# A fused attention and MLP kernel on one core: PSUM banks from one table, batch 0's leftover q and k through GpSimd, and remade instruction orders

## The chip, the core and the metric

The kernel runs on one core of a Trainium2 chip. The metric is device time in microseconds (us), as the median of several runs of one kernel. Engines are written PE (TensorE matmul), PEld (its weight loads), DVE (VectorE), ACT (ScalarE), POOL (GpSimd) and SP (SyncE). A run is called slow below when it lies more than 1.5% above the fastest run of the same kernel, and fast otherwise; comparisons use fast runs alone.

## The reference

Two stages, f32 in and f32 out. First a Performer attention with 128 random features, for 8 batches, 8 heads, 576 rows and 64 columns per head; then an MLP with a sigmoid gate over all 4608 rows.

```python
def phi(x):                                    # x is q or k, scaled by 64 ** -0.25
    proj = einsum('bhsd,md->bhsm', x, omega)   # 64 -> 128 features
    h = proj - sum(x * x) / 2
    h = h - max(h, axis=-1)
    return exp(h) / sqrt(128)

kv  = einsum('bhsm,bhsd->bhmd', phi(k), v);  z = sum(phi(k), axis=2)
num = einsum('bhsm,bhmd->bhsd', phi(q), kv);  den = phi(q) . z + 1e-6
x   = (num / den) as (4608, 512)

h   = x @ w_in                                 # 512 -> 2048
out = (h / (1 + exp(-1.702 * h))) @ w_out      # 2048 -> 512
```

## The kernel before

The program is a graph of some 1,530 operations. Three tables, made beforehand, say how it runs: `ORDER` is the fixed sequence of each engine, `BANK` names the PSUM bank of each accumulation group, and the waits are derived from data, buffers and banks. An engine that waits for one operation holds everything after it in its list.

```python
def schedule(self):
    self.order = {e: [ops[i] for i in ORDER[e]] for e in ENGINES}
    names = iter(BANK)
    for op in ops:
        for gr in op.opens:
            gr.bank = next(names)          # one of H0 H1 O0 O1 P0 P1 S0 S1
    ...                                    # a group waits for the bank's last group

def emit(self, name, eng, sems):
    for op in self.order[name]:
        for n, v in self.waits[op.i]:
            eng.wait_ge(sems[n], v)
        ...                                # then the instructions of op
```

576 rows are four blocks of 128 and a rest of 64, which the kernel calls the *leftover* and packs for all heads into tiles of its own (QL for q and k, VL for v). In batch 0 its q and k come over SP as f32 into QLF and are cast by DVE:

```python
def load_ql(b, key, ckey, after=()):
    pool = b >= QL_SW                      # QL_SW = 2: batches 0 and 1 over SP
    ...
    g.add(POOL if pool else SP, lambda e, dst=dst, so=so: e.dma_start(dst, so), ...)
    ...
    fv = lambda e: e.tensor_copy(out=QL[s][:, :, :, :], in_=QLF[s][:, :, :, :])
```

From there runs a chain that every V group (phi(k) times v, the sum over rows) of the batch needs: transpose on PE, copy to TL, projection with omega, maximum per row (NML, on DVE), exp of it (WWL, on ACT), mask and product with v on POOL (WWM, VPL).

The MLP has two stages for each batch. In stage 1, 16 groups of four 512-column matmuls each go through a tanh on ACT and a multiply on DVE into GT. In stage 2, four blocks of 128 rows accumulate 16 matmuls each; ACT copies a block into one of four output buffers, OS, and SP issues the output.

```python
NQK, NV, NTT, NQP, NVP, NO, NTH, NGT, NOUT = 2, 2, 4, 4, 4, 4, 3, 2, 4
...
gr, os_ = Group(POOL_OF["O" if sbi < 7 else "Oend"], False), m % NOUT
...
g.add(ACT, lambda e, ...: e.activation(out=OS[os_][:, :], in_=at(gr, 0, 512)(), func=ACTF.Copy, scale=0.5), ...)
g.add(SP, lambda e, ...: e.dma_start(dst, OS[os_][:, :]), ..., reads=[("os", os_)], ...)
```

The SP list holds the DMA transposes (TT and TL from loaded q and k, XT from attention's result OO) from batch 2 on.

## Time and profile before

| | before |
|---|---|
| time, median of the runs given at first | 324.06 us (323.75 to 324.21) |
| span of the profiled run | 321.7 us |
| PE busy | 307.4 us (96%) |
| first projection / first V / first stage 1 / first stage 2 starts | 9.48 / 15.85 / 26.50 / 41.44 us |
| last matmul ends | 317.7 us |

The prediction below shows the shares, the stretches, the waits and both ends. Two more places turn out to matter. The first is where the leftover chain of batch 0 ends, in the timeline (start, duration, engine, source line, operation, output from input, form; in brackets the idle time before it and what ended it):

```profile
13.37 1.04 POOL L683 TENSOR_TENSOR VPL<-VL,WWM 128x512 bf16<-128x512 f32 x1
...
15.85 0.42 PE L427 MATMUL PB<-VP,QKP 128*128 128x65 bf16 x8 [0.73 <-ACT QKP L641]
```

The product with v is done at 14.4 us, and what PE waits for before the first V group at 15.85 is an exp on ACT, not the leftover. The second place is the SP queue with the first outputs, in the timeline, and the busy times of the stretch from 100 to 120 us (PE, weight loads, DVE, ACT, POOL, clock, DMA share, GB/s):

```profile
77.70 0.83 SPq L1003 DMA_DIRECT2D out_dram<-OS  x2
78.64 6.08 SPq L762 DMA_TRANSPOSE TT<-QK  x2
```

### The profile page before, as it was taken

The numbers are of one execution on the slowest core, as the hardware profiler recorded it, in microseconds if no ns is written. First come the engines' busy times: TensorE is split into PE (matmuls) and PEld (weight loads), VectorE is DVE, ScalarE is ACT, GpSimd is POOL, SyncE is SP. The second block draws the span as 40 slices with busy tenths as digits, with TensorE's granted clock in tenths as the row PEclk, the third lists the DMA queues.
The fourth block names the chain that finished last, engine by engine and source line by source line (L and its number), as shares of the span: only waits on it lengthen the run. The fifth ranks groups of instructions, "written<-read, shape, count | busy, mean of one in ns | idle before, by whom it ended". The sixth has DMA issues, their size and how long they took to land.

```text
span 321.7 us, 5787 instructions
## 1 busy us (share of the span) xinstructions
PE 307.4 (96%) x2246; PEld 151.2 (47%) x2246; DVE 190.7 (59%) x401; ACT 187.3 (58%) x378; POOL 113.1 (35%) x185
## 2 busy tenths in 40 slices
PE   1798999999999999999999999999999999999994
PEld 1574554445544544454454544454544444444442
DVE  0899985368656784686648745788574533342210
ACT  1789855489178646665658766686545543343231
POOL 6696283627019705933644364031200000000000
PEclk9999999999999999999999999999999999999999
DMA  7999999996889989998999999933022002011005
GB/s 134 241 226 222 207 210 222 151 145 129 209 163 206 226 120 162 245 193 155 141 159 194 207 158 168 151 99 61 2 41 86 0 2 98 33 67 65 33 17 148
DMA packets 84119, 44.20 MB, mean 137 GB/s; under 512 B 54844, under 2 KB 77756, under 8 KB 84092
## 3 DMA queue, kind: packets, MB, share of 16 engines
q0 software_dynamic: 29792, 20.45, 42.0%
q1 hardware_dynamic: 54300, 23.37, 35.4%
q8 instruction: 18, 0.29, 0.4%
q14 instruction: 9, 0.07, 0.1%
HBM read 36.73 MB, written 9.44 MB: 144 GB/s over the span
## 4 chain that ended last, share of the span: by engine, by line
PE 86%; ACT 5%; DVE 5%; DMA 2%; issue 1%; POOL 1%; POOLq 0%
PE HT L427 36%; PE OB L427 34%; PE PB L427 11%; PE SB L427 4%; ACT QKP L641 3%; DMA QK<-in_q_dram 2%; DVE GT L966 1%; DVE NM L631 1%; ACT TH L961 1%; DVE OO L855 1%; ACT QKL L641 1%; POOL QK L478 1%; DVE TT L598 0%; DVE RD L847 0%; PE PB L868 0%
## 5 line engine op out<-in xcount | busy, mean ns | idle before, releaser
L966 DVE SCALAR_TENSOR_TENSOR GT<-TH,HT 128x512 bf16<-128x512 f32 x144 | 97.8, 683 | 80.4 <-ACT TH L961 80.0
L427 PE MATMUL HT<-XT,WIN 128*128 128x512 bf16 x576 | 142.2, 379 | 0.6 <-DVE GT L966 0.3
L961 ACT ACTIVATE TH<-HT 128x512 f32<-128x512 f32 x144 | 86.2, 600 | 82.7 <-PE HT L427 74.9
L427 PE MATMUL OB<-WOUT,GT 128*128 128x512 bf16 x496 | 122.5, 379 | 0.0
L427 PEld LDWEIGHTS HT<-XT,WIN 128*128 128x128 bf16 x576 | 52.7, 98 | 61.5 <-DVE GT L966 7.7
L427 PEld LDWEIGHTS OB<-WOUT,GT 128*128 128x128 bf16 x496 | 45.7, 98 | 53.4 <-issue 3.4
L780 POOL TENSOR_TENSOR VP<-VS,WW 128x512 bf16<-128x512 f32 x32 | 33.5, 1050 | 38.8 <-ACT WW L774 38.7
L641 ACT ACTIVATE QKP<-PB 128x512 bf16<-128x512 f32 x54 | 31.4, 600 | 7.2 <-PE PB L427 4.1
L641 ACT ACTIVATE QKP<-SB 128x512 bf16<-128x512 f32 x56 | 33.0, 606 | 2.8 <-PE SB L427 1.1
L995 ACT ACTIVATE OS<-OB 128x512 f32<-128x512 f32 x31 | 18.6, 599 | 16.7 <-PE OB L427 16.6
L631 DVE TENSOR_REDUCE NM<-SB 128x4 f32<-128x512 f32 x31 | 20.9, 682 | 8.8 <-PE PB L427 7.4
L631 DVE TENSOR_REDUCE NM<-PB 128x4 f32<-128x512 f32 x23 | 15.5, 683 | 6.9 <-PE PB L427 5.3
L427 PE MATMUL PB<-WOUT,GT 128*128 128x512 bf16 x80 | 19.4, 379 | 0.0
L478 POOL DMA_DIRECT2D QK<-in_k_dram x17 | 13.4, 790 | 7.1 <-DMA QK<-in_q_dram 4.2
L789 POOL CAST VP<-WW 128x8 bf16<-128x8 f32 x32 | 7.0, 225 | 24.3 <-ACT WW L774 24.3
L855 DVE TENSOR_TENSOR OO<-PB,RD 128x320 bf16<-128x320 f32 x29 | 13.7, 485 | 0.4
L478 POOL DMA_DIRECT2D QK<-in_q_dram x17 | 13.0, 768 | 0.0
L503 POOL DMA_DIRECT2D QL<-in_k_dram x12 | 7.8, 649 | 13.6 <-DMA TT<-QK 13.6
L427 PEld LDWEIGHTS PB<-WOUT,GT 128*128 128x128 bf16 x80 | 7.8, 98 | 9.5 <-DVE GT L966 0.3
L855 DVE TENSOR_TENSOR OO<-SB,RD 128x320 bf16<-128x320 f32 x24 | 11.5, 482 | 0.3
L532 POOL DMA_DIRECT2D VS<-in_v_dram x12 | 7.8, 661 | 7.2 <-DMA TT<-QK 7.2
L427 PE MATMUL PB<-TT,omB 64*128 64x512 bf16 (+1 forms) x31 | 10.2, 377 | 0.0
(140 smaller groups left out, 285.7 us busy)
## 6 DMA issues: line engine op xcount, KB each, us to landing
out_dram<-OS SPq DMA_DIRECT2D x32, 256.0 KB, 2.8
VS<-in_v_dram POOLq DMA_DIRECT2D x12, 512.0 KB, 6.6
QK<-in_k_dram POOLq DMA_DIRECT2D x15, 256.0 KB, 6.4
QK<-in_q_dram POOLq DMA_DIRECT2D x15, 256.0 KB, 7.3
WIN<-in_moe_w_in_dram POOLq DMA_DIRECT2D x4, 512.0 KB, 10.7
WOUT<-in_moe_w_out_dram POOLq DMA_DIRECT2D x4, 512.0 KB, 17.2
VS<-in_v_dram SPq DMA_DIRECT2D x4, 256.0 KB, 6.4
VS<-in_v_dram SPq DMA_DIRECT2D x2, 512.0 KB, 12.4
```

The costliest lines, as they stand in the source:

```text
L427: return lambda e: e.matmul(o() if callable(o) else o, lhsT=l, rhs=r, **kw)
L478: POOL, lambda e, dst=dst, so=so: e.dma_start(dst, so), 800, key,
L503: POOL if pool else SP, lambda e, dst=dst, so=so: e.dma_start(dst, so), 120, key,
L532: SP if b < V_SW else POOL, lambda e, dst=dst, so=so: e.dma_start(dst, so), 120, key,
L631: lambda e: e.tensor_reduce(out=o, in_=bass.AP(TILE[gr.bank], 0, [[512, 128], [128, 4], [1, 128]]), axis=AX.X, op=ALU.max, negate=True,),
L641: lambda e: e.activation(out=o, in_=view(gr, 0, pat or [[1, 512]])(), func=ACTF.Exp, scale=scale),
L780: lambda e: e.tensor_tensor(out=VP[vs][:, :, 0:64], in0=bass.AP(V, t * 9 * 64 + 64, [[NT * 9 * 64, 128], [64, 8], [1, 64]]), in1=bass.AP(W ...
L789: POOL, lambda e: e.tensor_copy(out=VP[vs][:, :, 64], in_=WW[vs][:, :]), 140, key + K_W + 240,
L855: lambda e, gr=gr, x=x: e.tensor_tensor(out=OO[os_][:, 5 * x : 5 * x + 5, :], in0=bass.AP(TILE[gr.bank], 0, [[512, 128], [65, 5], [1, 64]] ...
L961: lambda e, gr=gr, th=th: e.activation(out=TH[th][:, :], in_=at(gr, 0, 512)(), func=ACTF.Tanh, scale=0.851),
L966: lambda e, gr=gr, th=th, jc=jc: e.scalar_tensor_tensor(out=GT[gi][:, jc, :], in0=TH[th][:, :], scalar=1.0, in1=at(gr, 0, 512)(), op0=ALU. ...
L995: lambda e, gr=gr, os_=os_: e.activation(out=OS[os_][:, :], in_=at(gr, 0, 512)(), func=ACTF.Copy, scale=0.5),
```

## The change

The intent is to gain at the start (more banks, omega sooner, one cast less), to remove the two waits in the middle by orders made with a margin for late transposes and loads, and to shorten the end. Cut to its core:

```diff
-BANKS = dict(b0=<8 banks>, b1=<5>, b2=<5>, bv=<6>, H="H0 H1", O="O0 O1", Oend=<4>)
+BANKS = dict(b0=<8 banks>, b1=<8>, b2=<8>, bv=<6>, H=<8>, O=<8>, Oend=<8>)
-QL_SW = 2
+QL_SP = (1,)              # only batch 1's leftover q and k over SP; batch 0's over POOL, which casts
+TAIL = True
 ORDER = { PE: ... ACT: ... DVE: ... POOL: ... SP: ... }   # all five lists remade (cut)
 BANK  = ...                                               # remade over eight banks (cut)

+    def last_block(gi, key):           # the last 128 rows as two halves of 256 columns
+        for half in range(2):
+            ...                        # 16 matmuls of 256 columns, in 4 groups of 4
+            cut = 128 if half else 256
+            g.add(ACT, ... out=OS[os_][:, 0:cut], in_=at(gr, 0, cut)() ...)
+            if half:
+                g.add(DVE, ... out=OS[os_][:, 128:256], in0=at(gr, 128, 256)() ...)
+            for h in range(2):
+                g.add(ACT if half and h else SP, ... e.dma_start(dst, OS[os_][64*h : 64*h+64, 0:256]) ...)
 # cut: a halved leftover reduction that no batch uses; costs of the planner
```

The cast of batch 1's leftover moves from POOL to DVE in the new orders, and the first memset of the identity too.

## The prediction

> **What bounds the kernel now.** I read the page's shares first, then the busy time by stretch, then the waits of PE, then both ends in the timeline.
>
> ```profile
> PE 307.4 (96%) x2246; PEld 151.2 (47%) x2246; DVE 190.7 (59%) x401; ACT 187.3 (58%) x378; POOL 113.1 (35%) x185
> ...
> 0.00:8.00 8.00, 1.39 (x9) 0.82 (x9) 0.56 (x5) 1.42 (x2) 5.26 (x12) 1.00 0.70 134
> 8.00:16.00 8.00, 6.30 (x60) 4.53 (x60) 6.63 (x20) 6.03 (x16) 5.09 (x9) 1.00 1.33 242
> 16.00:24.00 8.00, 7.88 (x139) 6.27 (x136) 7.28 (x23) 6.89 (x17) 7.33 (x12) 1.00 1.25 226
> 24.00:32.00 8.00, 7.02 (x70) 3.67 (x67) 7.36 (x16) 7.47 (x17) 5.74 (x10) 1.00 1.26 223
> 32.00:40.00 8.00, 7.80 (x89) 4.26 (x88) 7.61 (x18) 7.25 (x17) 2.41 (x4) 1.00 1.24 207
> ...
> 240.00:260.00 20.00, 20.00 (x94) 8.96 (x93) 10.76 (x17) 10.15 (x17) 0.00 (x0) 1.00 0.16 43
> ...
> 310.00:322.00 12.00, 7.71 (x36) 3.33 (x34) 0.00 (x0) 2.98 (x5) 0.00 (x0) 1.00 0.43 111
> ```
>
> The columns after the stretch are PE, weight loads, DVE, ACT, POOL, clock, DMA share, GB/s. PE is at 96%, and from 40 us on it is never idle. But busy PE overlaps itself (a 512-column matmul lasts 379 ns and starts every 216), so I added up, from start to start, what exceeds columns / 2.4 GHz. The 576 + 576 MoE matmuls at 216 ns are 249 us; all PE work is 287 us. Excess after 40 us is 13 us, and almost all of it comes in equal steps that no order removes: 202 ns after each pair of 64-row projections (two run side by side, so this is their own time) and some 104 ns before one. Only two gaps are waits: 0.71 us at 179 us and 0.28 us at 94 us. Before 40 us it is another matter: first matmul at 5.67 us, then 7.2 us of excess to 20 us and 4.5 us to 40 us, of which I estimate 1.3 us as the cold clock and mode steps. So about 16 us are lost at the start, 1 us in the middle, and 4.0 us after the last matmul (317.7 to 321.7). In 8 to 40 us ACT (27.6 of 32 us) and DVE (28.9 of 32) are the full engines: here the kernel is bound by evacuating PSUM, with data still arriving. Only stage 2 of the MoE, whose first group starts at 41.4 us, gives PE work that needs little of either.
>
> ```profile
> PE OB L725 <- DMA QK<-in_k_dram: 5.7, 1, 5.7
> PE SB L725 <- DMA QK<-in_k_dram: 0.9, 1, 0.9
> PE PB L427 <- ACT QKP L641: 0.7, 1, 0.7
> PE HT L427 <- DVE TT L598: 0.6, 1, 0.6
> PE HT L868 <- DVE OO L855: 0.6, 1, 0.6
> ```
>
> These are the waits of PE: first for the q and k loads, later for ACT and DVE. Nothing else over 0.6 us is in that list.
>
> ```profile
> 0.73 0.81 SPq L491 DMA_DIRECT2D QLF<-in_q_dram  x1
> ...
> 1.60 0.62 SPq L491 DMA_DIRECT2D QLF<-in_k_dram  x1
> ...
> 2.91 0.46 SPq L446 DMA_DIRECT2D om_f<-in_omega_dram  x1
> ...
> 7.55 0.20 DVE L449 CAST om_raw<-om_f 128x64 bf16<-128x64 f32 x1 [6.58 <-DMA om_f<-in_omega_dram]
> 7.66 0.42 DVE L509 CAST QL<-QLF 128x512 bf16<-128x512 f32 x1
> ...
> 9.48 0.63 PE L427 MATMUL PB<-omB,TT 128*128 128x128 bf16 x4
> ...
> 316.02 0.60 ACT L995 ACTIVATE OS<-PB 128x512 f32<-128x512 f32 x1 [2.86 <-PE PB L427]
> 317.75 0.60 ACT L995 ACTIVATE OS<-PB 128x512 f32<-128x512 f32 x1 [1.13 <-PE PB L427]
> ```
>
> The timeline of both ends. Omega is fourth in the SP queue, behind two leftover loads and one of v; it holds DVE for 6.58 us, and the first projection starts only at 9.48. At the end one 0.60 us eviction follows the last matmul, then two output issues of 0.51 us one after the other, and the last lands 2.4 us after its issue, at 321.25.
>
> **What the Trainium skill says.** "DMA: Bandwidth & Descriptors", section "Issuing engines are not separate DMA queues": transfers from SP, ACT and GpSimd run on the same 16 engines and interleave. The trace agrees: from 2 us the completions of loads come as one stream, batch 0's q and k by 15.0, its last v at 15.0, the four WIN pieces at 22.7, 31.1, 33.7, 38.8, the WOUT pieces from 36.2 to 46.8, each 1 MB read in 2.6 us. Moving a load to another queue changes its turn, not the end of the stream. The same page, "SWDGE vs HWDGE vs iDMA": a cast during the DMA can only be issued from GpSimd. That is why batch 0's leftovers go there; the trace charges 0.77 us of POOL per such issue, against 0.62 to 0.81 on SP. "PSUM — Partial Sum Buffer", "Specifications (TRN2)", gives 8 banks, and no PSUM access for GpSimd: ACT and DVE alone empty them. In this trace too no POOL row reads one.
>
> **The change part by part.**
> *Bank table.* Before, stage 1 may use only H0 and H1, stage 2 only O0 and O1, attention of batches 1 to 7 five others. Now every group may take any of eight. No instruction is added. A stage 1 group holds its bank for 0.86 (PE) + 0.60 (tanh) + 0.68 (DVE) = 2.14 us plus handovers, against 0.86 us of PE per group: with two banks PE cannot run stage 1 alone at full speed (a group every 1.1 us or more). That matters only where stage 2 is not there to fill, in 26 to 41 us. There ACT and DVE have slack: over 8 to 40 us, 4.4 and 3.1 us. I count a third of the smaller: 1.0 us. After 40 us nothing is to be had from banks.
>
> *Batch 0's leftovers.* Two 128 KB f32 loads leave the head of the SP queue and become the 8th and 9th issues of POOL (counting the identity), and DVE's 0.42 us cast disappears; batch 1's 0.61 us cast moves from POOL to DVE at about 0.42, and one 0.23 us memset too. So DVE's total stays even. Omega is now second on SP, behind one load of v: an estimate from the stream (256 KB in about 1.3 us) lands it near 4 us in place of 7.5. The identity comes after five POOL issues: 1.24 + 5 x 0.77 + 0.3 = 5.4 us. k of pair 0 is the first load and should land near 5.6. So the first projection can start near 7.2 in place of 9.48: 2.3 us earlier for the ACT and DVE work behind it. But they are then fed by a stream whose last q and k of batch 0 still comes near 14 to 15 us, so I count 1.5 us.
> Against it: the leftovers land near 14.6 us (issued at 6.2 and 7.0, behind the rest of batch 0) in place of 5.8. Every V group of batch 0 reads the leftover v, scaled by the leftover k's maxima. Transpose 0.4, copy 0.6, projection 0.4, reduce 0.68, exp 0.2, two POOL products 1.3 and handovers make about 4.3 us, so V starts near 19 against 15.85 now. The new PE order has all batch 0 projections before V and more of batch 1 before the first stage 1 group (position 54 in place of 51), so this is partly covered; I charge 0.5 us.
>
> *New orders.* Batch 1's loads are gated on one q load, which was the fourth POOL issue and landed at 10.55 (POOL stood idle 4.17 us for it). It is now second, so this wait goes; but the DMA stream is full then, so it is worth nothing by itself. In the middle the margin can save at most the two waits, 1.0 us; I count 0.7.
>
> *Leftover split.* The code that halves the leftover reduction needs batch ≥ 1 and batch in (0,): it never runs. The descriptor counts and costs only serve the planner. Both cost nothing.
>
> *Tail.* The last 128-row block is computed as two 256-column halves, 32 matmuls of 108 ns in place of 16 of 216: no PE time, if the 98 ns weight loads keep up. The first half leaves while the second (1.73 us) runs. After the last matmul an eviction of 128 columns on ACT and one on DVE, side by side, take about 0.30 (estimate: half of 0.60) in place of 0.60; the two last issues go to SP and ACT at once, which saves 0.51; half the bytes save perhaps 0.1. Sum 0.9 us.
>
> Together: 1.5 + 1.0 - 0.5 + 0.7 + 0.9 = 3.6 us. 324.06 - 3.6 = 320.5 us.
>
> **Rivals.** (1) The late leftovers decide: V of batch 0 at 19 us or later, the first stage 1 group no earlier than now (26.5). For it speaks that ACT and DVE are short of other work until all loads are in. Then only banks, middle and tail are left, minus a little: about 322.5. (2) The start is better than I count: with all banks ACT and DVE run without a break from 6.5 us. Batches 0 and 1 and stage 1 of batch 0 cost them some 38 us each (my sum: per batch 18 exps of 0.60, 9 reductions of 0.68, about 9 copies of 0.5, 8 products of 0.485 and small ones, 28 us, so 14 each; 16 stage 1 groups of 0.60 + 0.68, 10 each), and half of their slack would become PE work; then 5 us at the start, and 318. Against it stand the serial chain in batch 0 and the load stream, which ends at 46.8 in any order. (3) A shared pool hurts: stage 2 accumulates over four groups and may hold several banks open, and a late transpose then blocks PE, whose order is fixed. The trace shows transposes landing 4.6 us after issue; one such stall a batch would cost 6 us and give 326. The orders were made with margin for just this, so I give it little.
>
> **Range and chances.** The end is sure within some 0.4 us, the middle within 0.7; the start carries the spread, from 0 to 5 us. Hence 317.8 to 323.2. Faster by over 2% needs under 317.6, about 6.5 us: 0.10. Slower by over 2% needs rival 3 on a large scale: 0.01.
>
> **What would show it.** Right: first projection between 6.8 and 7.8 us; first stage 1 group at 24 to 26 us; PE full from about 38; last eviction about 0.3 us and the span ending about 3.1 us after the last matmul; PE work unchanged at 287 us. Wrong: PE waits for DVE or POOL around 17 to 20 us (rival 1), or waits of more than 1 us after 60 us, for a transpose or a bank (rival 3); excess before 40 us, the wait for the first matmul included, under 13 us in place of 17.4 (rival 2; I expect 14 to 16).

## More of the kernel before

```profile
100.00:120.00 20.00, 20.00 (x173) 10.24 (x172) 15.51 (x37) 11.82 (x25) 10.34 (x17) 1.00 1.14 182
```

These two outputs (OS0 and OS3) leave just ahead of the next batch's transposes, and at 100 to 120 us PE is full, with a granted clock of 1.00. One output of batch 0 is late already here: the block in OS2 was evicted at 63.84 us, issued at 90.95 and landed at 93.76, 30 us later. It costs nothing, because the next eviction into OS2 starts only at 105.79.

## The result

| kernel | median us (range, runs) | fast runs against before's, same chip and rounds |
|---|---|---|
| before | 324.13 (323.75 to 324.37, 4) | |
| changed | 327.64 (326.66 to 333.22, 4; the 333.22 is slow) | 1.0092 [1.0063, 1.012] |

The changed kernel is 0.9% slower; the prediction was 1.1% faster and its range ended at 323.2. A ratio here is the mean time of one kernel's fast runs over the mean of the other's fast runs of the same rounds, so it isn't quite the ratio of the medians quoted, nor of all the runs listed (the plain means of experiment 1 would give 1.0114 in place of 1.0103); the brackets are its 95% interval. A fifth run of the changed kernel, 326.31 us and fast, counts in its ratio.

The profile that came with the changed kernel fell in the slow state. I therefore ran it again (first experiment), and show that run's profile. Two cautions on it: it is the longest of its six runs (330.94 us), and 38 of its matmul records are missing, so its PE busy sums are a little low. Both profiles of the changed kernel are thus of long executions (330.94 and 333.22 us); none of a typical one, near 327 us, was taken.

The page's shares and the stretches, against those shown of before:

```profile
PE 307.6 (93%) x2224; PEld 154.8 (47%) x2262; DVE 188.9 (57%) x398; ACT 187.3 (57%) x384; POOL 114.2 (35%) x185
```

```profile
8.00:16.00 8.00, 5.12 (x41) 3.99 (x40) 3.85 (x7) 2.78 (x7) 2.62 (x6) 1.00 1.22 218
16.00:24.00 8.00, 6.09 (x61) 4.09 (x59) 5.17 (x11) 7.52 (x19) 4.98 (x8) 1.00 1.26 243
...
100.00:120.00 20.00, 16.94 (x137) 8.61 (x139) 11.65 (x27) 10.51 (x22) 7.54 (x13) 0.91 0.97 194
```

The work is the same: all matmuls laid end to end by columns, as the prediction counts them, are 287 us before and 287 after (from the complete records of the slow profile). The lost time sits in two places. From 8 to 24 us DVE is busy 9.0 us (3.85 + 5.17) where it was 13.9 (6.63 + 7.28), and ACT in the first eight of these 2.78 where it was 6.03. And the stretch at 100 to 120 us, full before, has holes, at a clock of 0.91. The waits of PE say who is waited for:

```profile
PE SB L569 <- POOL ident L436: 5.6, 1, 5.6
PE SB L429 <- DVE GT L995: 2.9, 1, 2.9
PE PB L754 <- DMA QK<-in_k_dram: 1.7, 1, 1.7
PE PB L754 <- DMA QK<-in_q_dram: 1.2, 1, 1.2
PE HT L754 <- DMA QK<-in_k_dram: 1.0, 1, 1.0
PE OB L429 <- POOL VPL L723: 0.8, 1, 0.8
```

The first is the start-up, as before. The 2.9 us wait for DVE is the hole near 105 us. The others belong to the start: three waits for q and k, and one for VPL, the end of the leftover chain.

**The start.** The timeline, from omega's load to the first V group:

```profile
1.25 0.45 SPq L448 DMA_DIRECT2D om_f<-in_omega_dram  x1
...
3.83 0.48 DVE L451 CAST om_raw<-om_f 128x64 bf16<-128x64 f32 x1 [2.90 <-DMA om_f<-in_omega_dram]
...
8.23 0.63 PE L429 MATMUL OB<-omB,TT 128*128 128x128 bf16 x4
...
17.88 0.63 PE L774 MATMUL OB<-ident,QL 128*128 128x128 bf16 x4
...
21.13 1.04 POOL L712 TENSOR_TENSOR VPL<-VL,WWM 128x512 bf16<-128x512 f32 x1
...
22.48 0.42 PE L429 MATMUL OB<-VP,QKP 128*128 128x65 bf16 x8 [0.77 <-POOL VPL L723]
```

Omega is there at 3.8 us in place of 7.5, and the first projection starts 1.25 us sooner than before (9.48). But the leftover is transposed at 17.88 where it was 8.14, and V starts at 22.48 where it was 15.85, now released by POOL's VPL.

**The middle.** The SP queue and what follows from it, in the timeline:

```profile
91.05 1.28 SPq L907 DMA_TRANSPOSE XT<-OO  x1
...
95.56 1.05 SPq L1079 DMA_DIRECT2D out_dram<-OS  x2
...
103.54 0.60 ACT L1071 ACTIVATE OS<-HT 128x512 f32<-128x512 f32 x1 [3.21 <-DMA out_dram<-OS]
104.04 0.59 ACT L990 ACTIVATE TH<-OB 128x512 f32<-128x512 f32 x1
104.66 0.69 DVE L995 SCALAR_TENSOR_TENSOR GT<-TH,OB 128x512 bf16<-128x512 f32 x1 [5.91 <-ACT TH L990]
...
106.09 0.21 PE L429 MATMUL SB<-omB,TT 64*128 64x128 bf16 x1 [2.90 <-DVE GT L995]
```

The fourth block of batch 0 had been copied to its buffer, OS3, by 74.96 us (before: 74.10, issued at 78.09, landed at 84.96). SP issued its output only at 95.56, behind transposes that waited for their own data, and it landed at 103.46 among loads for the next batch. With four OS buffers, the block of batch 1 that uses this buffer next waits for that landing: ACT stands 3.21 us, the tanh behind it is late, DVE is late, and PE waits 2.90 us for the bank that DVE reads. After it the clock granted to PE is 0.50 from 107.4 to 110.8 us. In the slow profile of the same kernel the same chain is there: evicted 75.5, issued 96.29, landed 104.61, PE held for 3.5 us.

**The end.** From the last evictions on:

```profile
325.72 0.28 ACT L1023 ACTIVATE OS<-PB 128x128 f32<-128x128 f32 x1 [1.36 <-PE PB L429]
326.03 0.29 DVE L1031 TENSOR_SCALAR OS<-PB 128x128 f32<-128x128 f32 x1 [7.23 <-ACT OS L1023]
326.35 0.47 SPq L1041 DMA_DIRECT2D out_dram<-OS  x1
326.35 0.56 ACTq L1041 DMA_DIRECT2D out_dram<-OS  x1
```

The two halves of the last eviction take 0.28 and 0.29 us, but one after the other: DVE starts 0.31 us after ACT. The kernel's own rule makes the second access to a group wait for the first. The span ends 3.4 us after the last matmul (325.7 to 329.1); it was 4.0.

### The profile page after: what moved, and what is told of

Its sections match the earlier page's. It is cut to its first block, busy times and chain, and to the rows that moved or that the text cites. A ratio compares the mean times of both kernels' runs of the same rounds, so it can differ in the third digit from the quotient of the medians.

```text
span 331.4 us, 5832 instructions
## 1 busy us (share of the span) xinstructions
PE 311.3 (94%) x2262; PEld 155.8 (47%) x2262; DVE 188.8 (57%) x398; ACT 187.4 (57%) x384; POOL 114.2 (34%) x185
## 4 chain that ended last, share of the span: by engine, by line
PE 71%; DMA 18%; DVE 4%; ACT 3%; POOL 1%; SPq 1%; issue 1%; POOLq 0%; DVEq 0%; ACTq 0%
PE OB L429 20%; PE PB L429 18%; PE HT L429 17%; PE SB L429 16%; DMA TT<-QK 5%; DMA XT<-OO 3%; DMA WOUT<-in_moe_w_out_dram 3%; DMA out_dram<-OS 3%; DMA QK<-in_q_dram 2%; DMA QK<-in_k_dram 2%; DVE OO L884 1%; ACT QKP L645 1%; POOL QK L480 1%; DVE GT L995 1%; SPq L791 1%
## 5 line engine op out<-in xcount | busy, mean ns | idle before, releaser
L429 PE MATMUL OB<-WOUT,GT 128*128 128x512 bf16 x256 | 65.0, 383 | 0.0
L995 DVE SCALAR_TENSOR_TENSOR GT<-TH,PB 128x512 bf16<-128x512 f32 x41 | 28.0, 684 | 35.0 <-ACT TH L990 34.4
L429 PE MATMUL HT<-XT,WIN 128*128 128x512 bf16 x172 | 43.3, 379 | 0.0
L429 PE MATMUL PB<-XT,WIN 128*128 128x512 bf16 x164 | 41.7, 381 | 1.7 <-DMA XT<-OO 1.7
L995 DVE SCALAR_TENSOR_TENSOR GT<-TH,HT 128x512 bf16<-128x512 f32 x43 | 29.2, 682 | 18.1 <-ACT TH L990 17.9
L990 ACT ACTIVATE TH<-PB 128x512 f32<-128x512 f32 x41 | 24.5, 600 | 26.6 <-PE PB L429 22.5
L429 PE MATMUL SB<-XT,WIN 128*128 128x512 bf16 x148 | 37.5, 379 | 0.0
L990 ACT ACTIVATE TH<-HT 128x512 f32<-128x512 f32 x43 | 25.6, 601 | 20.1 <-PE HT L429 15.6
L995 DVE SCALAR_TENSOR_TENSOR GT<-TH,SB 128x512 bf16<-128x512 f32 x37 | 25.1, 681 | 12.3 <-ACT TH L990 12.2
L429 PE MATMUL SB<-WOUT,GT 128*128 128x512 bf16 x112 | 27.8, 379 | 0.0
L429 PE MATMUL PB<-WOUT,GT 128*128 128x512 bf16 (+1 forms) x128 | 27.2, 353 | 0.0
L990 ACT ACTIVATE TH<-OB 128x512 f32<-128x512 f32 x23 | 13.8, 601 | 20.5 <-PE OB L429 14.6
L429 PEld LDWEIGHTS HT<-XT,WIN 128*128 128x128 bf16 x172 | 15.7, 97 | 16.7 <-DVE GT L995 0.4
```

The lines of the kernel that those rows point to most:

```text
L429: return lambda e: e.matmul(o() if callable(o) else o, lhsT=l, rhs=r, **kw)
L990: lambda e, gr=gr, th=th: e.activation(out=TH[th][:, :], in_=at(gr, 0, 512)(), func=ACTF.Tanh, scale=0.851),
L995: lambda e, gr=gr, th=th, jc=jc: e.scalar_tensor_tensor(out=GT[gi][:, jc, :], in0=TH[th][:, :], scalar=1.0, in1=at(gr, 0, 512)(), op0=ALU. ...
```

## The experiments

The kernels ran in three calls, each on one chip with its own 11 runs of before (medians 324.17, 323.74 and 324.19 us); ratios are against these. All results were correct. Where only the lists of orders are edited, the diff says what moved. Experiments 1 to 4 make the first call, 5 to 8 the second, 9 to 12 the third. My theory at the outset: the loss has two parts, one at the start and one after 60 us; from experiment 5 on I took them for late leftovers and for outputs held in the SP queue. Rivals: the bank table, the held third load at the head of SP, or late transposes.

**1. The changed kernel again.** No edit.

> The changed kernel, unedited, for a profile in the fast state and a tighter ratio. Both theories: 326.3 to 328 us in fast runs, ratio 1.008 to 1.012. Theory A (the start lost about 2.5 us, the steady state about 1.5 us in fast runs, the tail won 0.6 us): the excess between matmul starts before 40 us is again about 20 us (17.4 in the kernel before), and the three waits of the slow profile after 60 us (1.8, 3.7 and 1.8 us) are there in part, 1 to 4 us in all. Rival B (the start is alone to blame, the waits after 60 us belong to the slow state): no wait of PE over 0.5 us after 60 us.

Measured: 328.57 us (326.24 to 330.94), ratio 1.0103 [1.006, 1.0147]. The result repeats. Of the three waits after 60 us in the slow profile one is there, of 2.9 us; the two for late transposes are not.

**2. The tail alone.** Before, with the new end only.

```diff
+TAIL = True        # last_block as in the change; before's orders otherwise
+                   # its 4 new operations at the ends of the lists, second half in bank H0
```

> The kernel before with nothing but the new tail (last block in two halves, last issues on SP and ACT). Theory A: 0.6 us off the tail, so 323.5 us, ratio 0.998. Rival (the tail is where the loss is, through weight loads that 256-column matmuls cannot cover or a slow ACT issue): same or slower, ratio 1.000 or more.

Measured: 324.17 us (322.75 to 324.85), ratio 0.9976 [0.994, 1.0012]. Before's median is the same 324.17, but its runs spread up to 326.58. The profile has 3.4 us after the last matmul in place of 4.0. So the profile puts the tail at 0.6 us, not 0.9; the ratio's 0.24% would be 0.8 us, but its interval includes 1.

**3. Old start, new rest.**

```diff
 # the change's kernel, with
-QL_SP = (1,)
+QL_SP = (0, 1)     # leftovers of batch 0 over SP again
 # ORDER: operations that before starts by 42.3 us in before's order, then the change's order
 # BANK: dealt anew over eight banks for these orders
```

> Orders up to 42.3 us from the kernel before (with its leftover loads on SP), everything later in the order of the change, with its tail and all eight banks. Theory A (both parts cost): 324.1 + 1.5 - 0.6 = 325.0 us, scattered by waits of PE for transposes. Rival B (only the start costs): 323.5 us, as with the tail alone. Rival C (only the steady state costs): 326 to 327.5 us, as the changed kernel.

Measured: 325.74 us (324.44 to 327.73), ratio 1.0032 [0.9991, 1.0073]. V is back at 16.20 us and stage 1 at 27.31. With the tail's 0.24% added back, the rest of the new orders costs 0.56%, 1.8 us; since the interval of either run is about 0.4% wide to each side, this difference is only just beyond the noise.

**4. New start, old rest.**

```diff
 # the change's kernel, with
-TAIL = True
+TAIL = False
 # ORDER: the change's order up to 40.5 us, then before's order
 # BANK: dealt anew over eight banks
```

> Orders up to 40.5 us from the changed kernel (leftovers by POOL), everything later in the order of the kernel before, with its tail, banks dealt anew over all eight. Theory A: 324.1 + 2.5 = 326.6 us. Rival B (only the start costs): 327.5 us. Rival C (only the steady state costs): 324 us.

Measured: 326.56 us (325.64 to 327.56), ratio 1.0055 [1.0019, 1.0091]; V at 21.19 us. The start costs 1.8 us (0.55% of 324.17). Start, rest and tail add up: 0.55 + 0.56 - 0.24 = 0.87%, where the whole change measured 0.92 and 1.03%.

**5. Seven output buffers** in place of four.

```diff
-NQK, NV, NTT, NQP, NVP, NO, NTH, NGT, NOUT = 2, 2, 4, 4, 4, 4, 3, 2, 4
+NQK, NV, NTT, NQP, NVP, NO, NTH, NGT, NOUT = 2, 2, 4, 4, 4, 4, 3, 2, 7
```

> The changed kernel with 7 output buffers in place of 4 (one number). Theory A2 (after 60 us the largest loss is a chain: an output issued late and landing late keeps its buffer, the next eviction by ACT waits for it, tanh behind it too, and PE waits for the bank, 3.1 to 3.7 us near 105 us plus some 1.7 us of cold clock after it): that wait and the clock dip go, mean granted clock 1.000, 323.5 to 326 us. Rival (transposes that land late behind loads hold PE by themselves): the wait near 105 us stays, 327 to 328.5 us.

Measured: fast runs 323.81, 324.06, 324.62 and 326.23 us, two slow ones at 330.12 and 331.63; ratio of the fast runs 1.002 [0.998, 1.0061] in place of 1.0103. The stretch with the hole, and the eviction that had waited:

```profile
100.00:120.00 20.00, 20.00 (x173) 10.24 (x171) 16.16 (x37) 10.98 (x20) 8.08 (x14) 1.00 1.16 194
```

```profile
97.95 0.62 ACT L1071 ACTIVATE OS<-HT 128x512 f32<-128x512 f32 x1
```

SP still issues the outputs late (at 92.41 us), but nobody waits for them: the eviction runs at once, and PE and its clock are full. So the output buffer, not the bank itself, made the hole. The size of the gain is less sure than its kind: the two slow runs are left out by the 1.5% rule, while 330.94 us of experiment 1 passes it. The four fastest runs of each have means of 327.8 and 324.7 us, but the plain means of all runs give ratios of 1.0114 and 1.0084. What is left in the fast runs, 0.20%, agrees with start and tail alone (0.55 - 0.24 = 0.31%).

**6. The leftovers alone.** Before, with batch 0's leftover loads as the 8th and 9th issue of POOL.

```diff
-        pool = b >= QL_SW
+        pool = b >= QL_SW or b == 0
 # orders: the two loads into POOL's list, the chain behind them moved back by hand to about 16 us
 # BANK: the first 35 groups dealt anew
```

> The kernel before, with batch 0's leftover q and k loaded by POOL (8th and 9th issue, after the identity), their transpose and what follows moved back in each order to about 16 us, banks of the first 35 groups dealt anew; nothing else. Theory A1 (the late leftovers hold V of batch 0, and with it the start): V not before 19 us in place of 15.85, first stage 1 group 1.5 to 2.5 us later than 26.5, 325.5 to 326.5 us. Rival (leftovers cost nothing by themselves, earlier omega pays for them; the loss at the start comes from the other moves in the new orders): 323.5 to 324.5 us.

Measured: 331.4 us (330.68 to 332.01), ratio 1.0227 [1.0197, 1.0257]: far worse than I expected.

```profile
16.00:24.00 8.00, 5.53 (x47) 4.29 (x47) 3.80 (x8) 3.22 (x8) 4.09 (x7) 0.50 1.22 254
```

```profile
21.06 0.62 PE L424 MATMUL HT<-VP,QKP 128*128 128x65 bf16 x8 [2.47 <-POOL VPL L691]
```

V starts at 21.06 us, after a wait of 2.5 us for VPL, and stage 1 at 34.5; ACT and DVE are starved, and the clock granted to PE is 0.50 in this stretch (from 16.0 to 26.3 us). My hand-made order may be worse than need be, so I take the 7.4 us for more than late leftovers have to cost in the old order. They show the direction; that the change's order recovers much of it is my reading of 1.8 us in experiment 4.

**7. The bank table alone.** Before's orders, banks dealt anew over all eight.

```diff
-BANK = """S0 S1 O0 P0 ...       # stage 1 in H, stage 2 in O
+BANK = """<dealt over H0 H1 O0 O1 P0 P1 S0 S1>
```

> The kernel before with its orders, and only the bank table made anew over all eight (each group takes the bank released first in the trace of before). Theory: with the orders fixed only two waits for banks, 0.47 and 0.30 us, can go: 323.3 to 324.2 us, ratio 0.998 to 1.000. Rival (sharing the banks itself makes stalls): over 325 us. Rival (banks are the gain that I predicted): 323 us or less.

Measured: 323.78 us (322.46 to 328.32, the 328.32 slow), ratio 1.0005 [0.9951, 1.0059]. The best estimate is nothing; the interval would still allow a gain of up to 0.5%. The run tells of before's orders only, not of orders made for eight banks.

**8. Omega first, with the tail.** Experiment 2 with the load of omega at the head of the SP list.

```diff
 SP: [
-        18, 17, 20, 7, 22, 21, ...
+        7, 18, 17, 20, 22, 21, ...     # 7 is omega; 18 and 17 are the leftovers of q and k
```

> The kernel before with the new tail and omega's load first on SP in place of fourth: a try for a version that beats both. If the wait of DVE for omega (6.58 us, until 7.5 us) is worth something, 322.5 to 323.2 us; if ACT, DVE and the loads bound the start anyway, 323.5 us as with the tail alone.

Measured: 323.59 us (322.77 to 324.12), ratio 0.9985 [0.9955, 1.0014], no more than the tail alone. The first projection started at 9.63 us, no earlier than before's 9.48: without the change's order of loads, something else keeps PE until then. So this run does not tell what an earlier projection is worth.

**9. Ungated loads first.** Experiment 5, with SP's list headed by omega, the leftover v and two loads of v, so that the load of v which waits for k no longer holds the queue from 1.7 to 5.3 us.

```diff
+NOUT = 7
 SP: [
-        v, omega, gated v, ...
+        omega, leftover v, v, v, gated v, ...
```

> The changed kernel with 7 output buffers (as e5) and five loads at the head of SP in another order: omega, leftover v, the two first loads of v, and only then the one that waits for the first load of k. In the changed kernel that one stands third and holds the SP queue until 5.3 us. Theory: leftover v and v come 3 to 6 us sooner, but V of batch 0 waits for the leftover k through POOL and that comes as late as before, so at most 0.5 us better than e5: 323.5 to 324.5 us. Rival (the held SP queue leaves the stream of loads idle, and this is the loss at the start): 1 us or more better than e5, 322.5 to 323 us.

Measured: 325.47 us (324.36 to 327.41), ratio 1.0048 [1.0014, 1.0081]. That is later than either theory had it. V starts at 21.0, no sooner than in experiment 5 (20.23); the held queue was not what made the start slow. The loads moved ahead delayed others: the first three q and k loads of batch 0 landed at 6.34, 8.00 and 9.16 us in place of 5.32, 6.14 and 6.84, and the first projection starts at 9.61 where it is 7.58 in experiment 5. The ratio is 0.28% higher, 0.9 us, with overlapping intervals; the projection's two microseconds and V's 0.8 are both in it, and nothing tells them apart.

**10. Old start, seven buffers.** Experiment 3 with NOUT = 7.

> e3 (old start, new rest, new tail, eight banks) with 7 output buffers: a try for a version that beats both. If start and output buffers are all that the change lost, 323.0 to 323.6 us, ratio about 0.997; if the new rest has a loss of its own in the late transposes, 324 to 325.5 us as e3.

Measured: 323.79 us (323.42 to 324.82), ratio 0.9988 [0.9964, 1.0012]. Against experiment 3 the buffers took off 0.44%, with intervals that overlap; against the changed kernel this version is 1.1% faster (0.9988 / 1.0103). Its runs are as close together as before's, without the scatter up to 330 us.

```profile
16.00:24.00 8.00, 7.40 (x125) 5.67 (x123) 7.31 (x21) 7.40 (x18) 7.31 (x13) 1.00 1.26 221
```

DVE is back at 7.31 us in 16 to 24 us (7.28 before, 5.17 changed), and PE is busy for all of 100 to 120 us. The profile of experiment 3, its fastest run, already had no such stop: two evictions waited 0.56 and 0.49 us for outputs to land, and PE was not held for over 1 us by them. So how large the hole is differs from run to run.

**11. Outputs earlier in SP's list.** The change with its four buffers, three outputs of batch 0 moved ahead of the first transpose of batch 3.

```diff
 SP: [
-        ..., <transposes of batch 3>, ..., out(OS2), out(OS1), out(OS3), ...
+        ..., out(OS2), out(OS1), out(OS3), <transposes of batch 3>, ...
```

> The changed kernel with 4 buffers, and three output transfers of batch 0 moved up in the SP order: their data lie ready at 64.7, 65.5 and 75.5 us, and SP issues them at 97.6, 93.3 and 96.3, behind transposes; now they stand before the first transpose of batch 3. Theory A2 (the late output is what holds ACT and PE near 105 us): the wait and the clock dip go without more buffers, 324 to 326 us, as e5. Rival (only the number of buffers matters, or the outputs now delay the transposes): 327 us or more.

Measured: fast runs 324.72 to 329.19 us, one slow at 332.18; ratio 1.0068 [1.0027, 1.011]. The hole is gone from its profile (PE 20.00 of 20 in 100 to 120 us), so the place in SP's list is a cause. But in the fast runs this recovered 0.35% where seven buffers recovered 0.83%, with intervals that overlap: between the two expectations. A wait of 1.2 us for a late XT transpose remains near 161 us.

**12. Tail and seven buffers.** Experiment 2 with NOUT = 7, the control for 5 and 10.

> Control: e2 (the kernel before with the new tail) with 7 output buffers. The trace of before has no wait of PE for an output, so no gain over e2: ratio 0.997 to 0.999. If it gains 1 us or more, the buffers were a loss in the kernel before too.

Measured: 323.75 us (322.48 to 324.89), ratio 0.9981 [0.9953, 1.001], against 0.9976 without. In before's order no gain from the buffers shows, so nothing speaks for their acting by some other way than through the late outputs. This and experiment 2 are the best versions that I found, about 0.2% below before, with 1 inside both intervals; none beats before for certain.

## Why the prediction was wrong

I predicted -3.6 us and measured about +3 us (0.92% of 324.13 is 3.0; experiment 1 gives 3.3). Step by step:

**The start, predicted 1.5 us gained with omega and 0.5 lost with the leftovers: in place of it 1.8 us lost (experiment 4, whose figure contains the banks too).** The events came as predicted at first: omega at 3.8 us, the first projection at 7.58 us in the slow profile and in experiment 5, at 8.23 in experiment 1. The step that failed is "this is partly covered; I charge 0.5 us". I had the chain's length nearly right: 4.3 us estimated, 4.6 measured (17.88 to 22.48, and 15.65 to 20.23 in experiment 5). It began later than the 14.6 us that I took: the second leftover landed at 15.1 us in experiment 5, 15.3 in the slow profile and 17.0 in experiment 1, and was transposed 0.6 to 1.2 us after that, behind other work in PE's list. V then starts at 20.2 to 22.5 us, not 19, and 4.4 to 6.6 us later than before. Until V runs, ACT and DVE run dry. I had named these as the full engines of this stretch and then counted an earlier first projection as their gain, without asking what they would have to do ten microseconds later. Experiments 3 and 6 show it from both sides: with the whole old start, leftovers on SP among it, V is back at 16.2 us and the start's loss is gone; with late leftovers alone in the old order, it is worse still. The earlier first projection is worth little (experiment 9 against 5: at most some 0.9 us for two microseconds, and not beyond the intervals). Stage 1 started 4 to 6.5 us later (30.5 us in experiment 5, 31.5 in the slow profile, 33.0 in experiment 1, against 26.5), and yet the start lost only 1.8 us of PE time. My reading, which no run isolates, is that the new order does more of batch 1's attention in the meantime. One difference I had overlooked: early in the span PE starts 128-column matmuls every 107 ns, later every 56, though the clock column reads 1.00 in both. The faster pace came at 12.3 us before and by 13.7 in experiment 5, but only at about 18 us in experiment 4, 19 in experiment 1 and past 21 in the slow profile. Summed over these matmuls I estimate 1.4 us before, 1.7 in experiment 5 and some 3 us in experiments 1 and 4. Experiment 5 lost time at the start all the same, so this is not the whole cause; how much of the 1.8 us it is, no run isolates.

**Banks, predicted 1.0 us: none measured in before's orders** (experiment 7). The term "I count a third of the smaller" was a share of slack, with no wait for a bank in the list of waits behind it.

**The middle, predicted 0.7 us gained: in place of it 1.8 us lost** (experiments 3 and 2, just beyond the noise). The step that failed is "the orders were made with margin for just this, so I give it little". I had rival 3 in hand, a late transfer that stops PE in a fixed order, and took the intent of the change for evidence. I also looked at the wrong transfer. Transposes do come late in single places, but the largest wait was for an output: SP's list puts outputs behind transposes, and four buffers are too few for an output that needs 28.5 us from eviction to landing (74.96 to 103.46) where before needed 11 for the same block (74.10 to 84.96). Late alone is not the harm, as the 30 us of another block before show; it is landing after the next eviction into that buffer is due. I read the outputs only at the end of the kernel. Experiment 5 settles the kind of this part: more buffers bring the ratio of the fast runs from 1.0103 to 1.002, and experiment 12 shows no gain from them in before's orders. The prediction's own sum agrees: the excess after 40 us is 13.1 us before, 21.0 in the slow profile of the changed kernel, and 12.4 and 13.3 in experiments 5 and 10, all from complete records.

**The tail, predicted 0.9 us: 0.6 in the profile** (experiment 2; the ratio cannot tell 0.6 from 0.9). The step was right in kind. One size was off: the two halves of the eviction run one after the other (0.28 and 0.29 us, DVE 0.31 later), so that this part of the gain is nil; what remains is the two issues at once and fewer bytes.

**Right:** the PE work is unchanged, and DVE's total stays even (190.7 to 188.9 us). One reading was off without consequence: of the 13 us of excess after 40 us, the steps around 64-row projections make not almost all but about half. Half of the 202 ns after a pair only balances what the sum credits for the pair's two matmuls starting 3 ns apart, and 3 us more are 3 ns for each matmul of 512 columns, which starts every 216 ns where 512 / 2.4 is 213.

**Of the rivals,** the first (late leftovers decide) and the third (a late transfer stops PE) both came, and each cost more than I gave it. The signs that I had written down for both were there: waits of PE for POOL at the first V, and a wait of over 1 us after 60 us. The excess before 40 us, which I expected at 14 to 16 us, was 18.9 in experiment 5, where before has 17.4.

**What stays open.** The runs of the changed kernel scatter more, in the changed kernel and in experiments 5 and 11, and some are slow ones at 330 to 333 us; experiments 10 and 12 show nothing like it, though experiment 7, with before's orders, has runs of 327.25 and 328.32. The profiles show single transposes that land late, but I have no pair of runs that ties the scatter to them, and slow runs prove nothing here. I also have not tried the new load order with the leftovers early, which might keep the earlier omega without its price. So within the new start, late leftovers are the cause that fits the waits and experiment 6, but the other moves of its order were not tested alone. The first piece of WIN, too, lands at 27.2 to 28.4 us in the kernels with the new start and at 22.7 to 23.8 in those with the old; no wait of PE in the profiles names it.

## What to carry to other kernels

Where two engines that drain PSUM are the full ones, ask of each load not when the first work can start but which later work all need it, and where in the fixed order its chain begins. An output costs nothing only as long as its buffer comes back in time: follow it from eviction to issue to landing, and compare that with the time of the next eviction into the same buffer, as soon as its queue also carries something that waits. And the purpose of a change ("with margin for late transfers") is not evidence that it has it.

## What the Trainium skill lacked or had wrong

- "DMA: Bandwidth & Descriptors", section "Issuing engines are not separate DMA queues", says that starting DMAs on several engines saves only the sequencer's time. It does not say what a waiting entry in one engine's list does to the ready ones behind it. Here an output whose block was evicted at about 75 us was issued at 95.56, 20 us later, and with it came a PE stop of 2.9 us; with the outputs moved ahead in the same list (experiment 11) that stop was gone.
- The same page, section "Latency and other measured facts", gives an HBM access 0.2 us on average and 2 us at high load, but no figure for a whole transfer among others. In experiment 1 an output of 256 KB took 2.9 us from issue to landing in the median, and 7.9 us (95.56 to 103.46) among the loads of the next batch: 5 us more.
- "TensorE: Matmul & The Clock Gate", section "Part 1: The HAM clock gate", gives an idle window of about 3.4 us after which the clock is halved. Shorter stops were enough here. In experiment 1 PE stopped for 2.90 us and resumed at 106.09 us; the granted clock was 0.85 in 106 to 108 us and 0.50 in 108 to 110, so the price came after work had resumed. In experiment 6 it fell to 0.50 at 16.0 us, and the longest stop of PE in the 7 us before that was 1.75 us (13.19 to 14.94).
